# Attention and FFN on one core: unscaled exponentials in the product with the values, inverse sums spread by DMA, and copies on any engine

## The chip, the cores and the metric

The kernel runs on one core of a Trainium2 chip. The metric is the device time of one execution in microseconds (us); lower is better. Times come from runs on the chip, rows from one profiled execution. The engines are TensorE (PE; PEld is its weight load), VectorE (DVE), ScalarE (ACT), GpSimd (POOL) and SyncE (SP), which issues the DMAs.

## The reference

Batch 8, 8 heads, 576 positions, head size 64; all in float32. First attention with a threshold, then an RWKV channel mix on its output `x` (8 x 576 x 512, hidden size 1024):

```python
scores = (1 / sqrt(64)) * (q @ k.T)
scores = where(scores >= max(scores) - tau, scores, -1e9)
attn = exp(scores - max(scores))
attn = attn / (sum(attn) + 1e-9)
x = (attn @ v) by heads, side by side
xk = mu_k * x + (1 - mu_k) * x_prev      # x_prev: x one position later, zero at first
xr = mu_r * x + (1 - mu_r) * x_prev
out = sigmoid(xr @ w_r) * (relu(xk @ w_k) ** 2 @ w_v)
```

## The kernel before

**Jobs.** A job is one batch and one pair of heads: 8 x 4 = 32 jobs. Its queries are taken in 5 units: four of 128 queries of each of the two heads, and one, "T", with the last 64 of both. A unit's scores (PE, L585 and L569) fill 128 x 576 of PSUM, in one of three buffers "s". DVE takes the negated maximum (L631) and adds tau (L639, "bias"); ACT's Prelu with a huge slope (L647, "mask") frees the buffer and leaves every score under the threshold hugely negative; ACT's Exp (L655) gives the exponentials and, by an accumulator, their row sums. DVE adds 1e-9 and inverts (L663, L664), POOL multiplies the rows by the inverses (L678), DVE transposes in 32 x 32 blocks (L695; T: L699), and PE multiplies by the values (L724: 288 matmuls a job, in three pieces, into two "s" buffers). ACT copies the result to `xT` (512 positions) and `xE` (the last 64).

**Split floats.** PE takes `fp32r` operands, so each float32 operand is split into a rounded high half (a copy) and a remainder (a subtraction): ACT copies and POOL subtracts for K (L487, L495), ACT and DVE for Q (L505, L515, which also multiply by 0.125), ACT and POOL for the FFN's inputs (L845, L853) and its squared hidden layer (L888, L898). Weights come as 64-bit words and are turned into floats in four DVE steps (L412 clamp, L426, L433, L443) between ACT copies (L404, L450), with POOL's subtraction (L454).

**FFN.** When a batch's four jobs are done, its 512 positions are two chunks of 256; after batches 3 and 7 the last 64 positions of four batches make a third: 18 chunks. A chunk forms the difference of neighbours (L823), scales it (L832, twice for each of two halves of the channels and each of xk, xr), splits it, and runs 96 matmuls with w_k (L875), 24 with w_r (L917) and 48 with w_v (L939), with relu, square and split between (L883 to L898), a copy and sigmoid for r (L921, L925) and the final product (L945).

**Order.** Nothing is ordered by hand. Each step is added to a `Plan` with its engine, duration, buffers and a key; `Plan.order` simulates all engines and issues whatever can start first, ties by key. Keys are shifted by the tables NUDGE and FIRST. Steps of POOL and those DVE steps listed in PORT are kept from overlapping. The resulting order on each engine is fixed when the kernel is built; an engine waits for its next instruction's inputs even where a later one could run.

Of the kernel before, what the change touches and what calls it, by code (L numbers as in the profile page):

```python
# [7 lines left out]
F32 = mybir.dt.float32  # L8
# [8 lines left out]
TAU = 110.0  # L17
W_MIN = 2.0 ** (0x38 * 2 - 127)
# [24 lines left out]
class Step:  # L43
    __slots__ = (
        "eng", "occ", "lat", "fn", "key", "deps", "succ", "allocs", "idx", "missing", "ready",
        "start", "end", "kb", "soft", "att", "kind", "ni", "after",
# [3 lines left out]
class Plan:  # L50

    HOP, LATE, FROM, AHEAD = 0.05, 0.3, 200.0, 120.0
    SOFT = {"DVE": 0, "ACT": 0}
    NUDGE = {
# [8 lines left out]
    }  # L65
    FIRST, UNTIL = {
# [8 lines left out]
    PORT = {"dve5", "dve6", "dve7", "dve8", "dve7b", "dve14"}  # L75
    CHUNK, FETCH = 256, 3.55

    def __init__(self):
        self.steps = []
        self.tags = {}  # L80
        self.bufs = []

        self.soft = False
# [6 lines left out]
    def add(self, eng, occ, fn, reads=(), writes=(), key=0.0, lat=None, kb=0, wait=0.0, kind=None, ni=0, after=None):  # L90
        s = Step()
        s.soft = self.SOFT.get(eng, 0.0) if self.soft else 0.0
        s.att = eng == "PE" and key < -500
        early = (key + 1000 if s.att else key) < self.UNTIL
        if s.att:
            key += 1000 - self.AHEAD
        s.eng, s.occ, s.fn, s.kb, s.kind, s.ni, s.after = eng, occ, fn, kb, kind, ni, after
        s.key = key + self.NUDGE.get(kind, 0.0) + (self.FIRST.get(kind, 0.0) if early else 0.0)
        s.lat = occ + 0.1 if lat is None else lat
        s.idx = len(self.steps)  # L100
        s.deps, s.succ, s.allocs = set(), [], []
        s.ready = wait
# [36 lines left out]
    def order(self, loose=()):  # L139
        steps = self.steps  # L140
        for s in steps:
# [6 lines left out]
        for b in self.bufs:  # L148
            for u in set(b.users):
# [6 lines left out]
        open_ = {}  # L156
        for s in steps:
            free.setdefault(s.eng, 0.0)
            open_.setdefault(s.eng, set())
        for s in steps:  # L160
            if s.missing == 0:
                open_[s.eng].add(s.idx)
# [26 lines left out]
        while len(out) < total:  # L189
            best = None  # L190
            for e, cand in open_.items():
                f = free[e]
                pick = None
                for i in cand:
# [5 lines left out]
                    if e == "POOL" or s.kind in self.PORT:  # L200
                        t = max(t, port.get("DVE" if e == "POOL" else "POOL", 0.0))
                    late = t + s.soft
                    if s.after is not None:
                        late = max(late, s.after[0].start + s.after[1])
                    k = (late, s.key, i, t)
                    if pick is None or k < pick:
                        pick = k
                if pick is not None and (best is None or pick[0] < best[0]):
                    best = (pick[0], e, pick[2], pick[3])
            if best is None:  # L210
                raise RuntimeError("the plan is stuck")
            _, e, i, t = best
            s = steps[i]
            open_[e].discard(i)
            s.start = t
            if e == "POOL" or s.kind in self.PORT:
                port[e] = t + s.occ
            stall = 0.0
            if s.ni:
                more = self.CHUNK - code % self.CHUNK  # L220
                code += s.ni
                while more <= s.ni:
                    at = t + stall + s.occ * more / s.ni
# [3 lines left out]
            free[e] = t + s.occ + stall  # L227
            if e == "DMA":
                pipe = max(pipe, t) + s.kb / 260.0
                s.end = max(t + 3.5, pipe + 2.5)  # L230
            else:
                s.end = t + s.lat + stall
# [11 lines left out]
            for j in s.succ:  # L244
                n = steps[j]
                n.missing -= 1
                same = n.eng == e and e == "PE"
# [123 lines left out]

# [671 lines left out]
```

## Time and profile before

| | |
|---|---|
| median of 3 runs | 991.8 us (991.47 to 992.29) |
| span of the profiled execution | 992.1 us |
| busy: PE, ACT, DVE, POOL | 896.4, 797.4, 700.8, 576.3 us |
| DMA | 97.48 MB, 31,599 packets |

The span is what a profiled execution shows from its first to its last instruction; no other time is given for that execution, and its span lies within the three runs. Busy time is the union of an engine's instructions, which overlap by some tens of nanoseconds; so the sum of a group's durations is a little more than what it adds to the busy time. A matmul's end is modelled; "idle before" counts only time in which nothing of that engine was under way.

### The profile page before, as it was taken

To read this page: it belongs to the slowest core of one execution; us is meant where nothing else is said; L and a number is where in the kernel's file an instruction comes from. 1 tells how busy PE (TensorE), PEld (TensorE's weight loads), DVE (VectorE), ACT (ScalarE), POOL (GpSimd) and SP (SyncE) were. 2 spreads that over 40 slices of the span, in tenths; PEclk is the share of its full clock that TensorE was granted. 3 is DMA by queue.
4 is the path that set the end of the run, shared out by engine and by line. 5 is a ranking of instruction groups with operands and counts; after the bars stand their busy time and mean duration, and the time that the engine had idled before them with its cause. 6 is when DMAs were issued, how large, how long until landed. Compare 5 with 4: busy or idle time off the path is not lost.

```text
span 992.1 us, 32003 instructions
## 1 busy us (share of the span) xinstructions
PE 896.4 (90%) x13520; PEld 785.9 (79%) x13520; DVE 700.8 (71%) x1434; ACT 797.4 (80%) x1660; POOL 576.3 (58%) x576
## 2 busy tenths in 40 slices
PE   4255668999999999999999999999999999999988
PEld 3154557888888979898989887989888988889876
DVE  6999889886778786878677877696778676731130
ACT  6677897889898988998888888989988888864432
POOL 2556575755676564766666656666575565553431
PEclk9577787999999999999999999999999999999999
DMA  9632232332333233233323232323333321100001
GB/s 339 263 109 75 78 127 63 123 128 84 89 126 109 74 105 116 90 108 96 119 94 122 84 101 91 95 82 98 118 98 107 97 96 62 71 3 22 22 22 22
DMA packets 31599, 97.48 MB, mean 98 GB/s; under 512 B 3808, under 2 KB 3808, under 8 KB 27360
## 3 DMA queue, kind: packets, MB, share of 16 engines
q1 hardware_dynamic: 31456, 95.44, 29.4%
q8 instruction: 106, 1.74, 0.7%
q14 instruction: 37, 0.30, 0.1%
HBM read 85.99 MB, written 9.44 MB: 96 GB/s over the span
## 4 chain that ended last, share of the span: by engine, by line
PE 65%; DVE 16%; ACT 10%; issue 4%; POOL 2%; DMA 2%; SPq 0%; ACTq 0%; POOLq 0%; DVEq 0%
PE w L875 16%; PE s L724 15%; PE w L939 14%; PE s L585 10%; PE w L917 8%; DVE sm L631 4%; ACT sq L647 3%; DVE sq L695 3%; ACT sq L655 3%; PE s L569 3%; DVE r L832 2%; DVE sm L663 1%; DVE qb L515 1%; POOL sq L678 1%; DMA wk<-in_w_k 1%
## 5 line engine op out<-in xcount | busy, mean ns | idle before, releaser
L678 POOL TENSOR_SCALAR sq<-sq,sm 128x576 f32<-128x576 f32 x288 | 233.0, 821 | 166.9 <-DVE sm L664 90.6
L631 DVE TENSOR_REDUCE sm<-s 128x1 f32<-128x576 f32 x288 | 211.5, 746 | 64.7 <-PE s L585 59.0
L647 ACT ACTIVATE sq<-s,sm 128x576 f32<-128x576 f32 x288 | 207.5, 740 | 46.5 <-DVE sm L639 43.9
L875 PE MATMUL w<-xk,wk 128*128 128x256 f32 x1728 | 227.9, 284 | 4.7 <-ACT xk L845 2.3
L655 ACT ACTIVATE sq<-sq,small 128x576 f32<-128x576 f32 x288 | 224.0, 780 | 1.8
L875 PEld LDWEIGHTS w<-xk,wk 128*128 128x128 f32 x1728 | 217.1, 190 | 9.1 <-issue 3.0
L939 PE MATMUL w<-wv,k 128*128 128x512 f32 x864 | 215.6, 394 | 0.0
L695 DVE STREAM_TRANSPOSE sq<-sq 128x1152 f32<-128x1152 f32 x128 | 175.3, 1371 | 40.8 <-POOL sq L678 40.4
L724 PE MATMUL s<-sq,v 32*64 32x144 f32 x9216 | 179.8, 294 | 13.1 <-ACT sq L647 5.0
L724 PEld LDWEIGHTS s<-sq,v 32*64 32x64 f32 x9216 | 151.9, 134 | 40.3 <-issue 20.3
L939 PEld LDWEIGHTS w<-wv,k 128*128 128x128 f32 x864 | 157.0, 188 | 32.3 <-issue 4.0
L585 PE MATMUL s<-kc,qa 128*128 128x288 f32 x512 | 124.2, 326 | 63.1 <-ACT sq L647 41.3
L585 PEld LDWEIGHTS s<-kc,qa 128*128 128x128 f32 x512 | 87.6, 200 | 88.1 <-ACT sq L647 43.7
L853 POOL TENSOR_TENSOR xk<-r,xk 128x512 fp32r<-128x512 f32 x72 | 94.2, 1308 | 80.3 <-ACT xk L845 74.8
L898 POOL TENSOR_TENSOR k<-r,k 128x512 fp32r<-128x512 f32 x72 | 93.7, 1304 | 53.8 <-ACT k L888 53.0
L585 PE MATMUL s<-kc,qb 128*128 128x288 f32 x512 | 115.2, 309 | 3.1 <-DVE qb L515 3.1
L495 POOL TENSOR_TENSOR kc<-rk,kc 64x576 fp32r<-64x576 f32 x64 | 92.8, 1461 | 40.7 <-issue 17.7
L917 PE MATMUL w<-wr,xk 128*128 128x512 f32 x432 | 108.9, 395 | 0.0
L832 DVE SCALAR_TENSOR_TENSOR r<-r,mu_sb,xT 128x256 f32<-128x256 f32 x128 | 65.3, 552 | 37.0 <-POOL xk L853 21.8
L585 PEld LDWEIGHTS s<-kc,qb 128*128 128x128 f32 x512 | 87.2, 200 | 4.6 <-DVE qb L515 3.8
L917 PEld LDWEIGHTS w<-wr,xk 128*128 128x128 f32 x432 | 77.9, 188 | 15.3 <-issue 1.0
L663 DVE TENSOR_SCALAR sm<-sm 128x2 f32<-128x2 f32 (+1 forms) x160 | 47.1, 294 | 53.9 <-ACT sq L655 53.5
(53 smaller groups left out, 914.3 us busy)
## 6 DMA issues: line engine op xcount, KB each, us to landing
v<-in_v SPq DMA_DIRECT2D x32, 1152.0 KB, 5.3
rk<-in_qk SPq DMA_DIRECT2D x64, 288.0 KB, 2.9
rq<-in_qk SPq DMA_DIRECT2D x64, 288.0 KB, 2.9
out<-sg SPq DMA_DIRECT2D x32, 256.0 KB, 2.3
wk<-in_w_k SPq DMA_DIRECT2D x8, 512.0 KB, 9.1
wv<-in_w_v SPq DMA_DIRECT2D x8, 512.0 KB, 10.2
wr<-in_w_r SPq DMA_DIRECT2D x4, 512.0 KB, 8.9
out<-sg SPq DMA_DIRECT2D x8, 128.0 KB, 2.4
```

The source lines that it names most:

```text
L585: PE.matmul(ss[y].get()[:, z, 0:HS], l.get()[:, c * P : (c + 1) * P], r.get()[:, keys(z)], start=(j == 0), stop=(j == 1),)
L631: lambda sv=sv, col=col: V.tensor_reduce(col(0), sv(), axis=AX.XY, op=ALU.max, negate=True),
L647: lambda st=st, pv=pv, col=col: A.activation(pv(), st(), AF.Prelu, bias=col(1), alpha=STEEP),
L655: lambda y=y, col=col: A.activation(part(y), part(y), AF.Exp, bias=small.get()[:, 3:4], accum_out=col(2)),
L678: lambda y=y: G.tensor_scalar(part(y), part(y), sm.get()[:, y, 3:4], 0.0, op0=ALU.mult, op1=ALU.add),
L695: V.transpose(t, t)
L724: PE.matmul(os[a // 2].get()[hs, a % 2, 0:NX], vt.get()[rows, j, hs], sq.get()[rows, j, h], start=(j == 0), stop=(j == NB - 1),)
L853: lambda j=j, d=d, cs=cs: G.tensor_tensor(mix[j].get()[:, 1, cs], d.get(), mix[j].get()[:, 0, cs].bitcast(F32), op=ALU.subtract),
L875: PE.matmul(h.get()[:, f], l, r, start=(ct == 0 and i == 0), stop=(ct == NCT - 1 and i == 2))
L898: lambda r=r, js=js: G.tensor_tensor(k2.get()[:, 1, js], r.get().rearrange("p (a b) -> p a b", a=2), k2.get()[:, 0, js].bitcast(F32), op=A ...
L917: PE.matmul(z.get(), l, r, start=(ct == 0 and i == 0), stop=(ct == NCT - 1 and i == 2))
L939: PE.matmul(vps.get(), l, r, start=(ft == 0 and i == 0), stop=(ft == NFT - 1 and i == 2))
```

## The change

The diff changes some 980 lines; this is its core.

- The exponentials are not normalized. DVE transposes them as they are, PE multiplies them by the values, and the result is multiplied by the inverse sums ("norm", "normt") after its copy from PSUM, once a job. The row sums of a job's 9 score tiles go into one tile `sums`, which starts as ones; one DVE step adds 1e-9, inverts and transposes it. A DMA writes it to DRAM ("line", 128 rows of 128 bytes), and four DMAs read it back so that each of 64 partitions of a head gets that head's inverses along the columns ("lines"). They land in a buffer of tag "raw", which four Q and K loads now share.
- The 0.125 moves from the split of Q to Prelu's `scale` and to the bias step. So Q's high half is a plain copy and its remainder a plain subtraction.
- A step may have several alternatives. Copies may go to ACT, DVE or POOL, two-input steps to POOL or DVE, a copy from PSUM, the relu and the copy for r to ACT or DVE, the clamp of weights and the bias to POOL or DVE; the plan takes whichever can start first, with a penalty for some (PEN), and new tables of keys (by kind and engine, and by job or chunk: GROUP).
- For batch 0 the product with the values fills one "s" buffer and both "w" buffers of the FFN in place of two "s" buffers. The third and later weights are requested by other keys.

```diff
-            add("DVE", 0.2, invert, reads=..., writes=..., key=n + 0.5, lat=0.38, kind="dve11")
-        for y in ys:
-            add("POOL", 0.72,
-                lambda y=y: G.tensor_scalar(part(y), part(y), sm.get()[:, y, 3:4], 0.0, op0=ALU.mult, op1=ALU.add),
...
+                        "bias", 0.11,
+                        lambda col=col, eng=eng: eng.tensor_scalar(
+                            col(1), col(0), SCALE, small.get()[:, 1:2], op0=ALU.mult, op1=ALU.add
...
+                        pv(), st(), AF.Prelu, bias=col(1), scale=SCALE, alpha=STEEP
...
+    def inverse(job, key):
+        total = job["sums"]
+        line = plan.buf(dr, "line", [P, Q], F32, 2)
+        inv = job["inv"] = sbuf("raw", [P, S], F32, NRAW)
+        def invert():
+            t = total.get()
+            V.tensor_scalar(t[:, 0, 0 : 2 * NCQ + 1], t[:, 0, 0 : 2 * NCQ + 1], 1e-9, None, op0=ALU.add)
+            V.reciprocal(t[:, 1, 0 : 2 * NCQ + 1], t[:, 0, 0 : 2 * NCQ + 1])
+            V.transpose(t[:, 1], t[:, 1])
+        add(dve("inv", 0.36, invert, lat=0.6), writes=[total], key=key)
+        add(dma("line", lambda: SY.dma_start(line.get(), total.get()[:, 1]), lat=2.2), reads=[total], writes=[line], ...)
+        for h in range(2):
...
+                SY.dma_start(inv.get()[rows, 0:SM].rearrange("p (a n) -> p a n", a=4), of.broadcast_to([D, 4, P]))
...
+                SY.dma_start(inv.get()[rows, SM:S].rearrange("p (a i) -> p a i", a=4), of.broadcast_to([D, 4, QT]))
...
+        add(pairs("norm", SM, whole, whole, lambda: inv.get()[:, 0:SM].rearrange(...), ALU.mult), ...)
+        add(pairs("normt", ST, end, end, lambda: inv.get()[:, SM:S], ALU.mult), ...)
...
+    def copies(kind, n, to, of, which="AVG"):
+        if "A" in which: r.append(act(kind, 0.094 + 0.000836 * n, lambda: A.activation(to(), of(), AF.Copy)))
+        if "V" in which: r.append(dve(kind, 0.067 + 0.00052 * n, lambda: V.tensor_copy(to(), of()), port=True))
+        if "G" in which: r.append(pool(kind, 0.08 + 0.00111 * n, lambda: G.tensor_scalar(to(), of(), 1.0, 0.0, ...)))
+    def pairs(kind, n, to, a, b, op, which="GV"):
+        if "G" in which: r.append(pool(kind, 0.08 + 0.00228 * n, lambda: G.tensor_tensor(to(), a(), b(), op=op)))
+        if "V" in which: r.append(dve(kind, 0.067 + 0.00104 * n, lambda: V.tensor_tensor(to(), a(), b(), op=op), port=True))
```

The tables move nearly every instruction. Three places show how.

DVE, in the first stage, around the fifth and sixth scale instruction on xT (L832), which feed the first FFN matmuls; before (L663 and L664 invert sums, L515 is Q's remainder, L639 the bias):

```order
L663 TENSOR_SCALAR sm_1437<-sm_1437 128x2
L664 RECIPROCAL sm_1437<-sm_1437 128x2
L631 TENSOR_REDUCE sm_1588<-s_1568 128x1
L631 TENSOR_REDUCE sm_1588<-s_1590 128x1
L639 TENSOR_SCALAR sm_1588<-sm_1588,small 128x1
L631 TENSOR_REDUCE sm_1611<-s_1598 128x1
L639 TENSOR_SCALAR sm_1588<-sm_1588,small 128x1
L639 TENSOR_SCALAR sm_1611<-sm_1611,small 128x1
L832 SCALAR_TENSOR_TENSOR r_1624<-r_1604,mu_sb,xT_68 128x256 x2
L515 SCALAR_TENSOR_TENSOR qb_1636<-rq_1075,small,qa_1576 128x576
L515 SCALAR_TENSOR_TENSOR qb_1639<-rq_1348,small,qa_1596 128x576
L631 TENSOR_REDUCE sm_1611<-s_1619 128x1
```

The same two scale instructions (L997) in the change; L709 is the maximum, L720 the bias, L407 a copy, L424 a two-input step, L781 to L783 a job's inversion:

```order
L720 TENSOR_SCALAR sm_1574<-sm_1574,small 128x1
L424 TENSOR_TENSOR xE<-xE,raw_1308 128x64
L980 TENSOR_TENSOR r_1585<-xT_70 128x512
L407 CAST kc_1589<-raw_1515 128x576
L997 SCALAR_TENSOR_TENSOR r_1591<-r_1585,mu_sb,xT_70 128x256 x2
L424 TENSOR_TENSOR kc_1589<-raw_1515,kc_1589 64x576
L407 CAST xk_1016<-r_1591 128x512
L709 TENSOR_REDUCE sm_1612<-s_1596 128x1
L709 TENSOR_REDUCE sm_1619<-s_1577 128x1
L781 TENSOR_SCALAR sums_76<-sums_76 128x9
L782 RECIPROCAL sums_76<-sums_76 128x9
L783 STREAM_TRANSPOSE sums_76<-sums_76 128x32
```

The pairs of inversions are gone, one triple stands for a whole job, and DVE now copies and subtracts for K, scales `xE` by the inverses, forms the difference and makes the high half of xk itself.

POOL, up to the low half of xk that the first FFN matmuls wait for (L853), before; L678 normalizes:

```order
L495 TENSOR_TENSOR kc_1579<-rk_1283,kc_1579 64x576
L823 TENSOR_TENSOR r_1604<-xT_68 128x512
L771 TENSOR_SCALAR xE<-xT_68 128x4
L678 TENSOR_SCALAR sq_1317<-sq_1317,sm_1437 128x18x32 x2
L495 TENSOR_TENSOR kc_1608<-rk_1323,kc_1608 64x576
L678 TENSOR_SCALAR sq_1317<-sq_1317,sm_1588 128x18x32 x2
L853 TENSOR_TENSOR xk_1213<-r_1624,xk_1213 128x512
```

The same low half (`xk_1016`, L422) in the change; L494 clamps weights:

```order
L422 TENSOR_TENSOR qb_1544<-raw_1391,qa_1540 128x576
L422 TENSOR_TENSOR xT_70<-xT_70,raw_1308 128x4x4x32
L413 TENSOR_SCALAR bd<-qb_1544 128x4x16
L422 TENSOR_TENSOR wv_0_1551<-xT_72,wv_0_1551 128x512
L494 TENSOR_SCALAR xT_72<-xT_72 128x512
L422 TENSOR_TENSOR xk_1016<-r_1591,xk_1016 128x512
```

Normalizing is gone from POOL; a scaling by the inverses (`xT_70<-xT_70,raw_1308`), Q's remainders and clamps are there in its place.

SP, the issues of one job's inverses in the change (there were none before), with the raw loads behind them:

```order
L792 DMA line_1290<-sums_80 128x32
L803 DMA raw_1308<-line_1290 64x4x128
L807 DMA raw_1308<-line_1290 64x4x16
L803 DMA raw_1308<-line_1290 64x4x128
L807 DMA raw_1308<-line_1290 64x4x16
L553 DMA raw_1373<-in_qk 128x576
L553 DMA raw_1382<-in_qk 128x576
```

The first waits for DVE's inversion, the second for the first to land, and the loads of Q and K are issued after both.

## Rows read from the trace of the kernel before

**Rows 1.** The page's part 1: busy us, share, instructions.
```profile
PE 896.4 (90%) x13520; PEld 785.9 (79%) x13520; DVE 700.8 (71%) x1434; ACT 797.4 (80%) x1660; POOL 576.3 (58%) x576
```

**Rows 2.** Busy time by stage (us from the start; instructions), granted clock, DMA.
```profile
0.00:157.60 157.60, 81.88 (x1380) 68.77 (x1381) 138.24 (x269) 118.86 (x254) 86.80 (x85) 0.72 0.46 162
...
175.00:870.00 695.00, 683.53 (x10895) 600.98 (x10882) 522.36 (x1069) 614.79 (x1296) 434.16 (x438) 1.00 0.31 99
...
917.00:992.00 75.00, 66.60 (x375) 58.44 (x373) 13.63 (x44) 23.84 (x38) 24.46 (x25) 0.96 0.07 22
```

**Rows 3.** PE's waits, 0 to 175 us: total, times, longest.
```profile
PE s L585 <- ACT sq L647: 39.3, 17, 11.6
```

**Rows 4.** Timeline around the first FFN matmul: start, us, instruction.
```profile
146.26 1.78 DVE L832 SCALAR_TENSOR_TENSOR r<-r,mu_sb,xT 128x256 f32<-128x256 f32 x2
148.27 0.62 ACT L845 ACTIVATE xk<-r 128x512 fp32r<-128x512 f32 x1
153.54 1.26 POOL L853 TENSOR_TENSOR xk<-r,xk 128x512 fp32r<-128x512 f32 x1
157.63 1.48 PE L875 MATMUL w<-xk,wk 128*128 128x256 f32 x6
```

**Rows 5.** DVE by line, 0 to 148 us: busy us, mean ns, idle before.
```profile
L631 DVE TENSOR_REDUCE sm<-s 128x1 f32<-128x576 f32 x46 | 33.9, 748 | 8.9 <-PE s L585 5.7 <-PE s L569 3.0
L515 DVE SCALAR_TENSOR_TENSOR qb<-rq,small,qa 128x576 fp32r<-128x576 f32 x12 | 11.8, 987 | 5.0 <-ACT qa L505 5.0
L412 DVE TENSOR_SCALAR xT<-xT 128x512 f32<-128x512 f32 x17 | 9.8, 590 | 0.4 <-ACT xT L404 0.3
L639 DVE TENSOR_SCALAR sm<-sm,small 128x1 f32<-128x1 f32 x46 | 9.1, 202 | 0.3
L443 DVE SCALAR_TENSOR_TENSOR xT<-wk,xT 128x512 uint32<-128x512 uint32 x8 | 8.2, 1020 | 0.0
L663 DVE TENSOR_SCALAR sm<-sm 128x2 f32<-128x2 f32 (+1 forms) x24 | 6.3, 263 | 0.3
L664 DVE RECIPROCAL sm<-sm 128x2 f32<-128x2 f32 (+1 forms) x24 | 4.0, 167 | 0.8
```

**Rows 6.** The tile xT on DVE, 0 to 160 us: ns, shortest, median, longest.
```profile
L426 DVE TENSOR_SCALAR xT<-xT x17: 405/422/1498, 13.2 to 139.8; 128x512 uint32<-128x512 uint32 x17
L433 DVE SCALAR_TENSOR_TENSOR xT<-wk,xT x8: 675/683/1114, 15.0 to 54.6; 128x512 uint32<-128x512 uint32 x8
```

**Rows 7.** Groups by line over the whole span: busy us, mean ns, idle before.
```profile
L678 POOL TENSOR_SCALAR sq<-sq,sm 128x576 f32<-128x576 f32 x288 | 233.0, 821 | 166.9 <-DVE sm L664 90.6 <-DVE sm L639 25.8 <-ACT sq L655 9.9
L515 DVE SCALAR_TENSOR_TENSOR qb<-rq,small,qa 128x576 fp32r<-128x576 f32 x64 | 58.5, 926 | 5.0 <-ACT qa L505 5.0
L663 DVE TENSOR_SCALAR sm<-sm 128x2 f32<-128x2 f32 (+1 forms) x160 | 47.1, 294 | 53.9 <-ACT sq L655 53.5
L945 DVE TENSOR_TENSOR sg<-w,sg 128x512 f32<-128x512 f32 x36 | 24.5, 680 | 49.0 <-issue 32.9 <-PE w L939 16.0
```

**Rows 8.** Timeline at 36 us, a pass of POOL and one of DVE.
```profile
36.48 1.59 POOL L454 TENSOR_TENSOR wk<-xT,wk 128x512 fp32r<-128x512 f32 x1
36.87 1.49 DVE L426 TENSOR_SCALAR xT<-xT 128x512 uint32<-128x512 uint32 x1
```

**Rows 9.** The chain of waits, four long pieces of PE: start, us, line.
```profile
882.50 1.71 PE s L724 x96
897.85 11.48 PE w L875 x96
909.33 5.50 PE w L917 x24
976.67 10.89 PE w L939 x48
```

**Rows 10.** The page's part 6: DMA issues, KB each, us to landing.
```profile
v<-in_v SPq DMA_DIRECT2D x32, 1152.0 KB, 5.3
out<-sg SPq DMA_DIRECT2D x8, 128.0 KB, 2.4
```

More of the change, by code (lines that the diff above doesn't have):

```diff
@@ L246, in order @@
                 n.missing -= 1
-                same = n.eng == e and e == "PE"
+                same = e == "PE" and n.alts[0][0] == "PE"
                 late = self.LATE if n.att and t > self.FROM else 0.0
-                n.ready = max(n.ready, t + s.occ + stall if same else s.end + self.HOP + late)
+                n.ready = max(n.ready, t + occ + stall if same else s.end + self.HOP + late)
                 if n.missing == 0:
-                    open_[n.eng].add(j)
+                    release(n)
             out.append(i)
@@ new lines, in dma @@
+    def dma(kind, fn, lat=3.5):
+        return ("DMA", DQ, lat, fn, kind, False)
+    def copies(kind, n, to, of, which="AVG"):
+        r = []
+        if "A" in which:
+            r.append(act(kind, 0.094 + 0.000836 * n, lambda: A.activation(to(), of(), AF.Copy)))
+        if "V" in which:
+            r.append(dve(kind, 0.067 + 0.00052 * n, lambda: V.tensor_copy(to(), of()), port=True))
+        if "G" in which:
+            r.append(
+                pool(
+                    kind,
+                    0.08 + 0.00111 * n,
+                    lambda: G.tensor_scalar(to(), of(), 1.0, 0.0, op0=ALU.mult, op1=ALU.add),
+                )
+            )
+        return r
@@ L359, in tile_threshold_attention_then_rwkv_ffn @@
+    add(dve("tau", 0.4, threshold), reads=[(small, 0)], writes=[(small, 1), (small, 3)], key=-1000)
     mu_sb = fixed("mu_sb", [P, 2, NCT])
@@ L711, in attend, with bank @@
         tail = [(xE, (b % NE, hp))]
-        os = [psum("s", [P, 2, 512], 3) for _ in range(2)]
         last = job["units"][-1]
-        for o in os:
-            add("PE", 0.0, lambda: None, reads=[(last["sm"], (RES, 1))], writes=[o, *main, *tail], key=-400.0, lat=0.0, kind="pe4")
+        if job["ji"] < NPAIR:
+            os = [psum("s", [P, 2, 512], 3), *(psum("w", [P, 512], NF) for _ in range(2))]
+            groups = [(os[0], 0, 2), (os[1], 2, 1), (os[2], 3, 1)]
+        else:
+            os = [psum("s", [P, 2, 512], 3) for _ in range(2)]
+            groups = [(os[0], 0, 2), (os[1], 2, 2)]
+        def bank(o, z):
+            return o.get()[:, z] if o.tag == "s" else o.get()
+        where = {a + z: (o, z) for o, a, m in groups for z in range(m)}
+        for o in os:
+            add(
+                pe("hold", 0.0, lambda: None, lat=0.0),
+                reads=[(last["sm"], (1, 1))],
+                writes=[o, *main, *tail],
+                key=-400.0,
+            )
         for k in range(KC):
@@ new lines, in attend, with whole, end @@
+        inv = job["inv"]
+        def whole():
+            return rows(x.get()[:, hp, 1 : 1 + SM])
+        def end():
+            return xE.get()[:, hp, b % NE, 1 : 1 + ST]
+        add(
+            pairs(
+                "norm",
+                SM,
+                whole,
+                whole,
+                lambda: inv.get()[:, 0:SM].rearrange("p (a c i) -> p a c i", a=4, i=Q),
+                ALU.mult,
+            ),
+            reads=[(inv, (0, h)) for h in range(2)],
+            writes=main,
+            key=key - 5,
+        )
@@ L767, in edge @@
+        add(
+            pairs("normt", ST, end, end, lambda: inv.get()[:, SM:S], ALU.mult),
+            reads=[(inv, (1, h)) for h in range(2)],
+            writes=tail,
+            key=key - 5,
+        )
     def edge(b, key):
         add(
-            "POOL",
-            0.16,
-            lambda: G.tensor_scalar(
-                xE.get()[:, :, b % NE, 0:1], xT[b % 2].get()[:, :, SM : SM + 1], 1.0, 0.0, op0=ALU.mult, op1=ALU.add
+            copies(
+                "edge",
+                NCT,
+                lambda: xE.get()[:, :, b % NE, 0:1],
+                lambda: xT[b % 2].get()[:, :, SM : SM + 1],
@@ new lines, in two @@
+            def two(r=r):
+                return r.get().rearrange("p (a b) -> p a b", a=2)
+            add(
+                [
+                    act("relu", 0.478, lambda r=r, flat=flat: A.activation(r.get(), flat(), AF.Relu), lat=0.6),
+                    dve("relu", 0.6, lambda r=r, flat=flat: V.tensor_scalar(r.get(), flat(), 0.0, None, op0=ALU.max)),
+                ],
+                reads=[h],
+                writes=[r],
+                key=key - 20,
+            )
+            add(
+                [
+                    act("sqr", 0.52, lambda r=r: A.activation(r.get(), r.get(), AF.Square)),
+                    *pairs("sqr", 512, lambda r=r: r.get(), lambda r=r: r.get(), lambda r=r: r.get(), ALU.mult),
+                ],
+                writes=[r],
+                key=key - 1,
+            )
```

712 lines of the change are left out of this document (415 added, 297 removed), and 29 rows, old and new, of tables (GROUP, NUDGE).

## The prediction

> **What bounds the kernel now.** I read the page's shares first, then busy time by stage, then TensorE's (PE's) waits, then VectorE (DVE) alone in the first stage. PE is busy 90% of the span, ScalarE (ACT) 80%, DVE 71%, GpSimd (POOL) 58% [rows 1]; such an average hides where PE stands still. By stage [rows 2]: up to 157.6 us, where the first FFN matmul of xk with w_k starts, DVE is busy 138.2 us of 157.6 (88%) and PE 81.9, at a mean granted clock of 0.72. From 175 to 870 PE is busy 683.5 of 695, so it stands still for 11.5 us; beside it ACT works 614.8 (88%) and DVE 522.4 (75%). After 870 only FFN chunks are left, and PE is still idle for 8.4 of the last 75. So PE sets the time after the start; in the start the softmax chain does. The longest waits there say it: PE waits 39.3 us for the ACT mask to free a score bank [rows 3], and ACT got its bias from a DVE with little time to spare. By PE's order 228 score matmuls (0.13 us each: 288 columns against the 256 of L875, which take 0.12 [rows 9]) and 1,152 of the product with the values (0.018 each [rows 9]) lie ahead of the first FFN matmul: 50 us of work spread over 157.6. That is the place to win.
>
> **The start, on DVE.** Up to the sixth "scale" instruction on xT (L832; it ends at 148.0, [rows 4]) the order before and the order now hold nearly the same work on DVE: 46 maxima, 18 + 5 transposes, 16 weight tiles' last two steps. So only the difference counts, priced from DVE's own rows up to 148 us [rows 5]. Removed: 24 pairs of sum and reciprocal, 6.3 + 4.0 us; 11 fused q remainders at 987 ns, 10.9; 15 of 17 weight clamps, which go to POOL, at 590 ns, 8.9; 9 of 46 biases, also to POOL, at 202 ns, 1.8. Together 31.9.
> Added, between the shortest and the longest price that a like row shows:
> - 9 copies (7 of 576 columns, 2 of 512). A one-input pass over 512 columns takes 422 ns at the median [rows 6] and 589 on average [rows 5]: 4.1 to 5.8.
> - 7 two-input passes over 512 columns (5 weight remainders, a difference, a scaling by the inverses): 683 ns at the median [rows 6] to 950, just under the 1020 of the dearest row [rows 5]: 4.8 to 6.7.
> - 7 of 576 columns (k and q remainders): 770 ns, the 683 scaled up, to 987: 5.4 to 6.9.
> - 4 triples that invert a whole job's sums, like the 263 + 167 ns of a pair plus one more small step: 1.9 to 2.8.
> - 4 scalings of 64 tail columns at 202 to 294 ns, like the small passes [rows 5, 7]; 4 copies out of PSUM, one of 256 and three of 128 columns, at 680 ns per 512 [rows 7] or half as much again: together 1.6 to 2.5.
> The sum is 17.8 to 24.7, so DVE is rid of 7 to 14 us. I take 11, nearer the good end, because POOL has less to do and collides less (below). The scale ends at 137 instead of 148.
>
> **From the scale to the first FFN matmul** before took 9.6 us, 148.0 to 157.6. POOL formed the low half only at 153.54 [rows 4]; in its order a k remainder and two normalizing passes stood ahead. Now a clamp alone stands ahead, and DVE makes the high half itself. At best it takes 0.8 + 0.4 + 1.3 = 2.5 us (a k remainder, the copy, POOL's 1.26), at worst 9.6 again. I take 4, near the low end, since what stood ahead is gone; PE's own row of score matmuls keeps it from less. The first FFN matmul comes at 141: **17 us earlier**. Eight score matmuls fewer lie ahead of it (220, 228 before), at 0.13 us each: 1 us back.
>
> **After it** PE has the same 13,520 matmuls in all. What moves is beside it. POOL loses its 288 normalizing passes, 233 us [rows 7]. Its two-input passes stay near their number (276 before, 263 now, 1.3 us each: 17 us less); 106 biases (21 us at DVE's 202 ns) and some 70 one-input passes at up to 821 ns (57 us) are new: 576 - 233 - 17 + 21 + 57 = 404. ACT hands some 340 of its copies, relus and squares on; at 0.6 us [rows 4] that is up to 200 of its 797. DVE gains: it loses 47 us of sums [rows 7] and 27 of reciprocals (160 at 167 ns [rows 5]), 58.5 of fused q remainders [rows 7], 21 of biases and 10 of clamps, and gets about 70 + 44 copies, 103 + 54 two-input passes and 54 + 36 reads of PSUM, by the prices above 240 to 286 us. So DVE goes from 701 to 776 to 823, and becomes the busiest engine after PE, near the 88% at which ACT stands there now. One nearly full neighbour takes the place of another: I take 3 of the 11.5 idle us (between all of them, and as many again lost). At the end the scaling by the inverses adds a step of 0.7 to 1.3 us ahead of the last batch's mix, while its halves may go to three engines: 2 us won, bounds 8 won and 5 lost. The DMAs (5 more a job, 160 in all) are costed at nothing: SP is no bound, and attention's own product covers them; if that cover is too short, see the third rival.
> **Sum:** 992.1 - 17 + 1 - 3 - 2 = **971 us**, 955 to 985 by these bounds when they don't all fall on one side. The profiled span, 992.1, lies within the three runs (991.47 to 992.29, median 991.8), so no correction.
>
> **A rule against it.** A DVE pass that began at 36.87 ended at 38.36, 0.29 us after POOL's pass that began at 36.48 [rows 8]; alone it takes 0.42 [rows 6]. It stood still for as long as POOL worked. The Trainium skill ("SBUF — State Buffer", Who interferes with whom) says why: DVE copies in a two-port mode, and DVE passes with two SBUF inputs, share a port pair with GpSimd, and the loser waits for the other's whole instruction. By that rule the two loads add up. POOL's falls by 172; such DVE passes grow by 122 to 168 (the 240 to 286, less some 50 of PSUM reads, less 58.5 + 10 removed). So the rule leaves the sum where it is, and only speaks against the place: POOL can wait, DVE can't. That is the second rival.
>
> **Rivals.**
> 1. *PE gains in the long stage too.* At the rates of undisturbed pieces (96 of L875 in 11.48 us, 24 of L917 in 5.50, 48 of L939 in 10.89, 96 of L724 in 1.71 [rows 9], scores 0.13) the matmuls from the first FFN matmul on need 207 + 99 + 196 + 144 + 137 = 783 us; they took 834.5. If ACT at 88% cost half of those 52: 992 - 16 - 26 = **950**. Against it: only 20 us show as idle, the rest lies inside rows of busy PE that this change leaves alone.
> 2. *Slower: collisions on DVE.* Some 580 DVE passes may now stand behind POOL (336 before), 520 of them ahead of the last maximum. At the shortest prices DVE's 776 us, less some 60 that its order now puts behind that maximum, are 716; with 19 idle in the start (157.6 - 138.2), today's 870 us are reached once each pass waits 0.26 us on average. For it: weight rows average 0.34 over their median (1020 against 682) [rows 5, 6]. Against it: POOL works 30% less, and by the median rows most passes wait for nothing. At 0.30 the stage ends at 716 + 156 + 19 = 891, 21 later than now: **1013**.
> 3. *The inverses come late.* They go to DRAM and back: a store of 128 KB lands in 2.4 us, a v tile in 5.3 [rows 10], so 5 to 8 us in all; behind the waiting issue stand the next raw loads on SP. In PE's order only 5 to 9 us of work stand between the end of attention and the first FFN matmul for batches 0, 3, 6 and 7. Five late us at each of the four: 971 + 20 = **991**. Against it: a job's product alone is 288 matmuls, 5.1 us at the rate of rows 9, and is issued in three pieces with other work between, all after the sums are known. The Trainium skill ("DMA: Bandwidth & Descriptors", Specifications) adds that pieces under 512 B cost a read-modify-write; the new rows are of 64 to 512 B, and no row here prices that.
> 4. *The start doesn't shrink*, as loads of weights and the chain max, bias, mask, exp set it and not DVE's sum: 4 us of 17 remain, **984**. For it: DVE's maxima wait 8.9 us there, mostly for PE [rows 5]. Against it: the other 138 us DVE is busy.
>
> **Chances.** Forecast 0.55; rivals 1 to 4: 0.20, 0.09, 0.06, 0.10. The range, 943 to 992, takes in rivals 1, 3 and 4 and leaves rival 2 and a little of both ends out. About 0.2%, 2 us, is what a measurement tells from no change: faster by more 0.87 (forecast, 1, 4 and a third of 3), within 0.04, slower by more 0.09.
>
> **What will show it.** Right: the first w_k matmul at about 141 us with DVE still near 88% busy before it; POOL near 404 us in all, ACT near 620, DVE near 800; PE idle in the long stage 10 us or less; no wait of a norm pass for a DMA on the chain. Wrong: w_k starting after 150 (rival 4), copies and remainders on DVE averaging 0.25 us over 0.42 and 0.68 (rival 2), PE or POOL waiting for the inverses' DMA (rival 3), PE's stage from its first FFN matmul to the end under 815 us (rival 1).

## The result: 0.7% slower

The changed kernel takes 1000.5 us (median of 10 runs, 993.8 to 1004.2) beside 992.5 for the kernel before (10 runs, 991.0 to 994.1): a ratio of 1.0069, 95% interval 1.0050 to 1.0089. The forecast was 971, the range ended at 992. The profiled execution spans 1000.6 us.

The page's part 1 of the changed kernel, and its busy time on either side of the first matmul with w_k (columns as in [rows 2]):

```profile
PE 906.1 (91%) x13520; PEld 793.5 (79%) x13520; DVE 791.0 (79%) x1445; ACT 642.1 (64%) x1321; POOL 408.1 (41%) x467
```
```profile
0.00:134.30 134.30, 78.65 (x1373) 65.69 (x1374) 117.61 (x217) 100.84 (x222) 63.58 (x78) 0.76 0.54 186
134.30:1000.60 866.30, 827.41 (x12149) 727.77 (x12148) 673.37 (x1229) 541.25 (x1101) 344.54 (x390) 0.98 0.31 95
```

The neighbours of PE carry what was forecast, and the start shrank by more than forecast: 134.3 us instead of 157.6 [rows 2]. All of that and more is lost behind it. The kernel before needed 834.5 us there (992.1 - 157.6), with PE busy for 814.5 (896.4 - 81.9, [rows 1, 2]); now it is 866.3, with PE busy for 827.4. So PE stands still for 19 us more and takes 13 us longer for the same matmuls, 12,149 of them here and 12,141 before. What PE waits for (whole span: total, times, longest):

```profile
PE s L847 <- issue: 28.4, 19, 4.1
PE s L652 <- ACT sq L734: 25.1, 20, 5.0
PE w L847 <- issue: 3.7, 2, 2.3
PE w L1149 <- issue: 2.7, 1, 2.7
```

"issue" is idle time for which the profile shows no wait: 34.8 us in all, 2.4 in the kernel before. Nearly all of it falls on L847, the product with the values. One such stall on PE's timeline, with score matmuls and w_k matmuls on both sides of it:

```profile
192.95 0.53 PE L652 MATMUL s<-kc,qa 128*128 128x288 f32 x2 [0.32 <-ACT sq L734]
193.32 0.42 PE L652 MATMUL s<-kc,qb 128*128 128x288 f32 x2
193.58 0.87 PE L1046 MATMUL w<-xk,wk 128*128 128x256 f32 x6
194.38 1.68 PE L847 MATMUL s<-sq,v 32*64 32x144 f32 x82
200.13 0.78 PE L847 MATMUL s<-sq,v 32*64 32x144 f32 x14 [4.07 <-issue]
200.84 0.85 PE L652 MATMUL s<-kc,qa 128*128 128x288 f32 x2
201.49 0.68 PE L652 MATMUL s<-kc,qb 128*128 128x288 f32 x2
201.97 1.27 PE L1046 MATMUL w<-xk,wk 128*128 128x256 f32 x5
```

PE stops in the middle of a piece of 96 and goes on 4 us later. Then it is slow as well: two score matmuls take 0.85 us instead of 0.53, five of w_k 1.27 where six took 0.87. The granted clock says why, 1.00 before the stall, 0.65 on average over the stall and the microseconds behind it, and 0.50 right behind it (last columns: granted clock, DMA share, GB/s). Of the chip's two levels, 2.4 and 1.2 GHz, PE was given the lower one for a time after it had stood still, so this stall is paid for twice:

```profile
186.00:196.00 10.00, 9.62 (x212) 8.02 (x212) 9.47 (x15) 8.31 (x18) 2.31 (x5) 1.00 0.46 118
196.00:204.00 8.00, 3.93 (x49) 3.26 (x56) 3.02 (x5) 1.39 (x4) 1.66 (x2) 0.65 0.37 108
200.13:204.00 3.87, 3.87 (x48) 3.26 (x56) 1.79 (x2) 0.56 (x1) 0.26 (x1) 0.50 0.05 14
```

What came just before, on SP's timeline (start, us to issue, line, DMA):

```profile
187.82 0.33 SPq L792 DMA_DIRECT2D line<-sums  x1
189.28 0.59 SPq L803 DMA_DIRECT2D raw<-line  x1
189.97 1.49 SPq L553 DMA_DIRECT2D raw<-in_qk  x3
191.51 0.59 SPq L807 DMA_DIRECT2D raw<-line  x1
192.14 0.74 SPq L803 DMA_DIRECT2D raw<-line  x1
192.93 0.93 SPq L807 DMA_DIRECT2D raw<-line  x1
193.91 1.18 SPq L1171 DMA_DIRECT2D out<-sg  x2
```

L792 stores a job's inverses, L803 and L807 spread them, L553 loads Q or K rows of the next job. SP waited for the sums, stored, waited again for the store to land, and then sent nine loads or stores more within 6 us. PE's instructions come over the same DMA engines, as queue q8. The DMA queues from 174 to 197 us (packets, MB, share) and, in the second fence, from 197 to 204:

```profile
q1 hardware_dynamic: 1861, 2.57, 37.3%
q14 instruction: 1, 0.01, 0.1%
```
```profile
q1 hardware_dynamic: 370, 0.54, 24.5%
q8 instruction: 2, 0.03, 2.4%
```

No packet of q8 ran from 174.9 to 197.2 us; then one did, up to 198.7, and PE went on at 200.1. Such a gap alone proves nothing: without the store and the loads (e_nodma, below) q8 is silent from 169.2 to 188.3, and PE has no stall put down to issue there. PE's own count does. q8 moved 106 packets of 16,384 bytes and PE ran 27,147 instructions (matmuls, weight loads, semaphore steps), 256 to a packet. Counted in their order in the trace, 21 of the 22 stops put down to issue, 33.7 of the 34.8 us, lie where one piece of 256 ends and the next begins, and each of the 15 of these that last over 1 us ends 1.2 to 1.5 us behind the end of a q8 packet. Other runs show the same: 4.5 of 5.6 us lie there in e_nodma, 11.2 of 12.2 in c_ldact5. So in these stalls PE waits for its own instructions. PE began the piece before the stall above at 191.76, and the packet with the next piece began only at 197.21; in between the DMA engines were 95% busy (last column but one):

```profile
191.76:197.21 5.45, 3.98 (x149) 3.31 (x135) 4.96 (x8) 3.71 (x9) 0.53 (x2) 1.00 0.95 261
```

Six more stalls of over 2 us behind this one follow the same cluster on SP. The DMA issues of the whole span (KB each, median us to landing), and SP's waits (total, times, longest):

```profile
raw<-in_qk SPq DMA_DIRECT2D x128, 288.0 KB, 4.9
raw<-line SPq DMA_DIRECT2D x64, 128.0 KB, 4.8
raw<-line SPq DMA_DIRECT2D x64, 16.0 KB, 4.9
```
```profile
SPq L792 <- DVE sums L783: 248.5, 28, 17.8
SPq L553 <- DMA raw<-in_qk: 33.1, 16, 4.3
SPq L803 <- DMA line<-sums: 32.5, 26, 2.8
```

Rows of Q and K now land in 4.9 us; in the kernel before in 2.9. DVE, ACT and POOL wait 47.4 us for them in all (15.4 before), the longest two groups here:

```profile
ACT qa L405 <- DMA raw<-in_qk: 18.6, 10, 3.7
DVE qa L407 <- DMA raw<-in_qk: 15.8, 9, 3.6
```

No engine but SP waits for the inverses or for their store.

### The profile page after: what moved, and what is told of

Its sections match the earlier page's. It is cut to its first block, busy times and chain, and to the rows that moved or that the text cites. A ratio compares the mean times of both kernels' runs of the same rounds, so it can differ in the third digit from the quotient of the medians.

```text
span 1000.6 us, 31601 instructions
## 1 busy us (share of the span) xinstructions
PE 906.1 (91%) x13520; PEld 793.5 (79%) x13520; DVE 791.0 (79%) x1445; ACT 642.1 (64%) x1321; POOL 408.1 (41%) x467
## 4 chain that ended last, share of the span: by engine, by line
PE 73%; DVE 15%; issue 5%; ACT 4%; DMA 2%; POOL 1%; SPq 1%; DVEq 0%; ACTq 0%; POOLq 0%
PE w L1046 18%; PE w L1149 17%; PE s L847 15%; PE s L652 11%; PE w L1115 8%; DVE sm L709 4%; DVE sq L762 3%; PE s L630 3%; DMA raw<-in_qk 2%; ACT sq L734 2%; ACT sq L746 1%; DVE xT L527 1%; DVE kc L424 1%; PE w L847 1%; DVE kc L407 1%
## 5 line engine op out<-in xcount | busy, mean ns | idle before, releaser
L709 DVE TENSOR_REDUCE sm<-s 128x1 f32<-128x576 f32 x288 | 209.7, 746 | 43.7 <-PE s L652 33.7
L847 PE MATMUL s<-sq,v 32*64 32x144 f32 x8640 | 189.9, 295 | 30.8 <-issue 28.4
L847 PEld LDWEIGHTS s<-sq,v 32*64 32x64 f32 x8640 | 156.4, 134 | 60.6 <-issue 50.8
L762 DVE STREAM_TRANSPOSE sq<-sq 128x1152 f32<-128x1152 f32 x128 | 173.6, 1362 | 11.6 <-ACT sq L746 11.5
L652 PE MATMUL s<-kc,qa 128*128 128x288 f32 x512 | 123.2, 324 | 43.8 <-ACT sq L734 25.1
L422 POOL TENSOR_TENSOR xk<-r,xk 128x512 fp32r<-128x512 f32 x72 | 98.2, 1364 | 156.5 <-DVE xk L407 114.3
L652 PEld LDWEIGHTS s<-kc,qa 128*128 128x128 f32 x512 | 90.5, 202 | 65.6 <-ACT sq L734 28.9
L652 PE MATMUL s<-kc,qb 128*128 128x288 f32 x512 | 116.0, 310 | 0.0
L1115 PE MATMUL w<-wr,xk 128*128 128x512 f32 x432 | 111.3, 399 | 0.0
L652 PEld LDWEIGHTS s<-kc,qb 128*128 128x128 f32 x512 | 87.8, 201 | 1.3 <-issue 1.2
L422 POOL TENSOR_TENSOR qb<-raw,qa 128x576 fp32r<-128x576 f32 x39 | 56.0, 1436 | 48.2 <-ACT qa L405 24.2
L997 DVE SCALAR_TENSOR_TENSOR r<-r,mu_sb,xT 128x256 f32<-128x256 f32 x128 | 60.2, 511 | 18.5 <-POOL xk L422 17.4
L720 POOL TENSOR_SCALAR sm<-sm,small 128x1 f32<-128x1 f32 x106 | 28.8, 273 | 102.2 <-DVE sm L709 92.9
L422 POOL TENSOR_TENSOR kc<-raw,kc 64x576 fp32r<-64x576 f32 x35 | 51.2, 1462 | 30.6 <-DVE kc L407 9.7
L1127 ACT ACTIVATE sg<-w 128x512 f32<-128x512 f32 x27 | 16.0, 594 | 72.2 <-PE w L1115 72.2
```

Of the source, the lines that this page charges most:

```text
L422: r.append(pool(kind, 0.08 + 0.00228 * n, lambda: G.tensor_tensor(to(), a(), b(), op=op)))
L652: PE.matmul(ss[y].get()[:, z, 0:HS], l.get()[:, c * P : (c + 1) * P], r.get()[:, keys(z)], start=(j == 0), stop=(j == 1),)
L709: lambda sv=sv, col=col: V.tensor_reduce(col(0), sv(), axis=AX.XY, op=ALU.max, negate=True),
L762: V.transpose(t, t)
L847: PE.matmul(bank(*where[a])[hs, 0:NX], vt.get()[rows, j, hs], sq.get()[rows, j, h], start=(j == 0), stop=(j == NB - 1),)
L997: V.scalar_tensor_tensor(d.get()[:, y, o : o + n], diff.get()[:, y, o : o + n], mu_sb.get()[:, j, hc + y : hc + y + 1], prv[:, hc + y], op ...
```

## The experiments

All kernels but the three named b_ are the changed one with an edit of its DMAs; on PE, DVE, ACT and POOL they keep its order of work, but for the instructions that an edit names. "Issue" is PE's idle time put down to issue, "rows" the time that DVE, ACT and POOL wait for Q and K rows, both in us of one profiled execution; the ratio is to the kernel before, run beside it on the same chip.

| run | edit | us | ratio (95%) | issue | rows |
|---|---|---|---|---|---|
| changed kernel | | 1000.5 | 1.0069 (1.0050 to 1.0089) | 34.8 | 47.4 |
| e_nodma | no store, no loads | 961.5 | 0.9695 (0.9669 to 0.9721) | 5.6 | 2.4 |
| e_store | store alone | 963.8 | 0.9705 (0.9675 to 0.9735) | 9.6 | 2.6 |
| e_free | loads alone | 962.6 | 0.9705 (0.9673 to 0.9736) | 7.3 | 7.1 |
| e_noland | both, no wait between them | 973.1 | 0.9826 (0.9788 to 0.9864) | 17.1 | 16.3 |
| e_fat | loads in long rows | 974.3 | 0.9828 (0.9786 to 0.9870) | 18.5 | 29.3 |
| e_rows | 5 stores, 2 loads in long rows | 988.1 | 0.9964 (0.9948 to 0.9980) | 17.5 | 72.3 |
| c_quad | 3 stores, long rows, 4 transposes | 992.8 | 1.0012 (0.9990 to 1.0035) | 15.5 | 25.8 |
| c_act | store and loads from ACT | 976.3 | 0.9837 (0.9808 to 0.9865) | 10.7 | 4.2 |
| c_ldact | loads from ACT | 973.6 | 0.9800 (0.9770 to 0.9831) | 13.0 | 6.9 |
| c_ldact5 | the same again | 971.8 | 0.9790 (0.9772 to 0.9807) | 12.2 | 6.2 |
| e_ldactfat | loads from ACT in long rows | 968.9 | 0.9756 (0.9724 to 0.9789) | 11.5 | 7.3 |
| c_actrows | e_rows, all from ACT | 1018.6 | 1.0265 (1.0239 to 1.0291) | 2.7 | 5.6 |

**First: is it the DMAs at all, and which property?** The theory was that their many small pieces hold up the loads of PE's instructions; its rivals, that PE's new order bunches the product by itself, and that SP waits for the sums and then sends everything at once, whatever the pieces.

e_nodma:
```diff
-    dma("line", lambda: SY.dma_start(line.get(), total.get()[:, 1]), lat=2.2),
-    SY.dma_start(inv.get()[rows, ...]...)   # four times a job
-    norm: x times inv
+    norm: x times x
```


> The change without any store or load of inverses; the scaling step multiplies the attention's output by itself, at the same size, so the scaling by the inverses is left out. Same order on PE, DVE, ACT and POOL. Theory 1: issue idle under 8 us, time 964 to 976. Theory 2: issue idle near 35 and 998 to 1002. Theory 3: SP no longer waits for the sums, 966 to 980. So this tells theory 2 from the others, and e_fat tells 1 from 3.

961.5 us, 39 less than the changed kernel (37 by the ratios): the spreading of the inverses costs more than the whole loss, and PE's new order alone bunches nothing. The two stretches of this run:

```profile
0.00:129.00 129.00, 78.60 (x1372) 67.17 (x1373) 116.61 (x217) 100.92 (x221) 63.05 (x78) 0.74 0.52 188
129.00:959.40 830.40, 814.06 (x12150) 718.68 (x12148) 672.66 (x1229) 539.48 (x1101) 342.90 (x390) 1.00 0.26 88
```

e_fat:
```diff
-    of = line...[:, :, NCQ * h * Q : NCQ * (h + 1) * Q]    # 4 pieces of 512 bytes a partition, and 4 of 64
+    of = line.get().rearrange("(o r) i -> o (r i)", o=1)[:, 0:SM]    # 1 piece of 2048, and 1 of 256
```


> The change with each load of inverses as one row a partition: 64 pieces of 2,048 bytes and 64 of 256 bytes in place of 256 of 512 and 256 of 64, twice a job; same bytes, same number of issues, same waits, same order on all engines. The values it spreads are not the inverses, so this leaves the right scaling out. Theory 1 (the many small pieces hold up PE's instruction loads): PE's idle time put down to issue falls from 35 us to under 10, the raw loads land in 3 to 4 us rather than 4.9, time 970 to 980. Theory 2 (PE's order bunches the product's pieces, so that it asks for instructions faster than they can come, whatever the DMAs do): issue idle stays near 35, time 998 to 1002. Theory 3 (SP waits for the sums and then issues loads in a burst; the number of bytes and issues counts, not that of pieces): issue idle 25 to 35, time 992 to 1001.

e_rows:
```diff
-    SY.dma_start(line.get(), total.get()[:, 1])
+    for a in range(4): SY.dma_start(line[:, a * P : (a + 1) * P]..., t[a * Q : a * Q + 2 * NCQ, 1])
+    SY.dma_start(line[:, SM:S]..., t[2 * NCQ :: Q, 1]...)
-    four loads of pieces of 512 and 64 bytes
+    SY.dma_start(inv.get()[rows], line.get()[h : h + 1].broadcast_to([D, S]))    # twice
```


> The change with the inverses stored so that each head's 576 lie in a row in DRAM: five small stores a job (40 pieces in all) and two loads of 64 pieces of 2,304 bytes, in place of one store of 128 pieces and four loads of 1,024. Computes all of the reference. Same order on PE, DVE, ACT and POOL. Theory 1: issue idle under 10 us, time 966 to 980, faster than the kernel before by 1 to 2.5%. Theory 2: 998 to 1002. Theory 3: six to seven issues a job remain in the same places, 990 to 1001.

b_small, the kernel before with four loads a job of 512 pieces in all per head (256 of 320 bytes, 256 of 64), nobody reading them:
```diff
-    lambda: SY.dma_start(vt.get(), v[b, hp]...),
+    lambda: (SY.dma_start(vt.get(), v[b, hp]...), extra(b, hp)),
```


> The kernel before, with four further loads a job, into a tile that nothing reads, issued right behind the load of the values: twice 256 pieces of 320 bytes and 256 of 64 bytes, as many pieces as the change has. Same order on all other engines. Theory 1: PE's issue idle rises from 2 to over 8 us, time 995 to 1012. Theory 2: nothing changes, 991 to 994. Theory 3: 991 to 995, since SP waits for nothing new.

b_small took 991.9 us, ratio 1.0009 (0.9994 to 1.0025), issue 2.4: as many small pieces as in the change cost nothing behind the load of v. So their number alone decides nothing. Long rows at the changed kernel's place won some 25 us (e_fat: 974.3), though SP waits for the sums there as before; so SP's wait alone doesn't either. e_rows, with the fewest pieces, won only some 11 (988.1): five stores a job make the Q and K rows later still, 72.3 us of waits for them.

**Second: wait or pieces?**

e_store keeps the store, e_free the loads, from the rows of Q and K:
```diff
# e_store
-    SY.dma_start(inv.get()[rows, ...]...)   # four times a job; norm: x times x
# e_free
-    dma("line", lambda: SY.dma_start(line.get(), total.get()[:, 1]), lat=2.2),
-    of = line...
+    of = qk[job["b"], job["hp"], h, 0:4, 0:P]...    # and 0:QT
```


> The changed kernel with the store of the inverses kept, so that SP still waits for each job's sums and for the store's buffer, but with its four loads left out; the norm passes multiply x by itself (the output is not the reference's). Theory A, that the loads' many small pieces, issued right when a job's sums are done, are what costs: close to the kernel without store and loads, 959 to 968 us, PE's idle time put down to issue at most 9 us. Theory B, that SP's wait for the sums is what costs, since it holds up the loads of the next job's rows and sends them in a burst: 975 to 1000 us, issue idle above 15 us.

> The changed kernel without the store: the four loads of a job stay at their places in SP's queue with the same pieces (512 and 64 bytes), but read the input rows, so that SP waits for no sums; the values are not the inverses. Theory A: the pieces still travel with the loads of the next job's rows, so 980 to 1000 us and issue idle above 15 us; lower within that the more the loads drift away from the product. Theory B: without the wait nothing bunches, 960 to 970 us, issue idle at most 9 us.

Both 963 us. In e_store SP waits for the sums as long as in the changed kernel; in e_free the same pieces go, in the same order on SP. Each alone costs 1 to 2 us over e_nodma, together they cost 39. Neither run has the second wait, that of the loads for the store to land, since that takes both. Both theories failed as they were put: A in e_free, B in e_store (whose issue idle, 9.6 us, lies a little above A's bound of 9).

b_hot is the kernel before with the change's store and loads behind each job's last inverse; b_hotfat the same in long rows:
```diff
     V.reciprocal(sm.get()[:, ysl, 3], sm.get()[:, ysl, 2])
+    if unit is unit["job"]["units"][-1]: extra(unit["job"], sm.get())    # copy, store, four loads
```


> The kernel before with a store of 128 rows and four loads of small pieces (256 of 288 bytes and 256 of 64 bytes, twice) per job, issued right behind the last inverse of a job's sums, the place that they have in the change; nobody reads them. Theory A (place and pieces) and theory B (SP's wait) both: 1000 to 1025 us, with PE's issue idle above 10 us. Theory C, that only the changed kernel's own order of work is open to it: 990 to 995 us and issue idle at most 4 us, as with the loads behind the v load.

> The kernel before with the same store and four loads per job at the same place as in the run with small pieces there (1003 us), but each load in long rows (64 of 1152 bytes and 64 of 256 bytes, twice). If SP's wait and the five DMAs cost, the number of pieces being of no account: 1000 to 1005 us. If the pieces cost: 990 to 997 us.

1003.3 us (ratio 1.0114, 1.0092 to 1.0136) and 1004.8 (1.0112, 1.0088 to 1.0136). Here the five DMAs with SP's waits cost 11 us whatever the pieces, and issue idle rises only to 5.7 and 5.8 us, not above 10. By the profiles b_hot is 8.9 us longer (1001.0 and 992.1): 1.6 lie in the start (its first w_k matmul comes at 159.2), 2.4 in PE standing still behind it and 4.9 in slower matmuls. What slowed these isn't settled.

c_quad computes all of the reference: four transposes into one block of partitions, so that long rows need three stores.
```diff
-    V.transpose(t[:, 1], t[:, 1])
+    for a in range(4): V.transpose(t[0:Q, 2 + a], t[a * Q : (a + 1) * Q, 1])
```


> The changed kernel with whole inverses in long rows and right values: four 32x32 transposes into one block of 32 partitions in place of one, a store of 8 rows of 512 bytes and two stores of 4 times 64 bytes, then four loads of long rows (64 of 2048 bytes, 64 of 256 bytes, twice). Theory A: 970 to 980 us, issue idle 14 to 20 us, as with the long rows of other values. Theory B: the two stores more lengthen SP's wait, 983 to 992 us, as with five stores.

992.8 us, a little above what B said, but not for B's reason alone: the four transposes cost as much on DVE as a large one each (its row of DVE's groups by duration: shortest, median, longest ns), 25.6 us in place of 6.8, and DVE's busy time rises to 811.9 us. This run mixes two causes and settles neither.

```profile
L784 DVE STREAM_TRANSPOSE sums<-sums x128: 199/200/204, 28.0 to 883.7; 32x32 f32<-32x32 f32 x128
```

**Third: take it out of SP's queue.**

c_act lets ACT's queue issue store and loads, c_ldact the loads alone:
```diff
-    SY.dma_start(inv.get()[rows, 0:SM]...)    # and [rows, SM:S]
+    A.dma_start(inv.get()[rows, 0:SM]...)
# c_act also
-    SY.dma_start(line.get(), total.get()[:, 1])
+    A.dma_start(line.get(), total.get()[:, 1])
```


> The changed kernel with the store of the inverses and their four loads issued by ACT's queue in place of SP's, everything else and every value the same: SP no longer waits for sums, ACT waits for DVE's inverses and for the store to land. Theory D, which the last runs leave: neither the pieces nor the wait costs by itself, but in SP's one queue the wait holds back the next job's row loads, so that they go together with the small pieces, at the moment when the product draws PE's instructions. D: the row loads go early again, issue idle falls below 15 us and the time to 962 to 978 us. Theory A, that the pieces just then are enough: 985 to 1000 us, issue idle above 20 us. Rival E: ACT's own waits hold up the mask and exponential passes, and PE waits for them: 980 to 1010 us with PE's waits for ACT above 25 us behind 175 us.

> The changed kernel with the four loads of the inverses on ACT's queue, as in the 976 us run, but with the store left in SP's, so that SP waits for a job's sums again before it gets to the next row loads. Theory D, that SP's wait holds back the row loads until they go together with the small pieces: 985 to 1002 us, row loads landing in 4.5 us or more, issue idle above 18 us. Theory F, that it is the loads' place in SP's queue, between the row loads, which then go through one queue behind the small pieces: 972 to 980 us and issue idle at most 13 us, as with all of them on ACT.

> The five small stores and two loads of long rows (the 988 us run), all issued by ACT's queue; right values. If the pieces still cost there: 964 to 974 us, issue idle at most 8 us. If ACT's waits and issues take the gain back: 976 to 990 us, with PE's waits for ACT's mask passes above those of the run with small pieces on ACT (7.6 us behind 175 us).

976.3 and 973.6 us; both compute all of the reference, and both are faster than the kernel before and the changed one. In c_ldact SP still waits for the sums, so D fell and F held: what matters is that the loads, and the wait for the store to land, stand in SP's queue ahead of the Q and K rows. c_actrows (e_rows, its stores and loads all from ACT) has hardly any issue idle left (2.7 us) and is the slowest of all, above either expectation: ACT, which has passes to run, waits for the stores to land, and PE for ACT's mask passes (25.4 us at L652 behind 175 us, 7.6 in c_act). Its rows of ACT's waits:

```profile
ACT sq L746 <- DMA line<-sums: 27.8, 10, 3.5
ACT sq L734 <- DMA line<-sums: 10.3, 3, 4.7
```

**Last: the wait for landing, or the queue?** e_noland is e_free with the store kept: SP waits for the sums, but the loads behind read rows of Q and K and so don't wait for the store. e_ldactfat is e_fat with its loads on ACT's queue.

> The changed kernel with its store kept on SP (which waits for the sums) and the four loads behind it, the same pieces, but reading the input rows, so that SP doesn't wait for the store to land; the values are not the inverses. F1, that this second wait holds the row loads back until they go with the pieces: 964 to 977 us, issue idle at most 14 us. F2, that small pieces ahead of the row loads in one queue are enough: 985 to 1000 us, issue idle above 20 us.

> Store on SP, the four loads on ACT's queue and in long rows (64 of 2048 and 64 of 256 bytes, twice; they spread values that are not the inverses). If pieces cost in a queue of their own too: 962 to 968 us, issue idle at most 10 us. If what is left there (974 us) is the waits and not the pieces: 971 to 976 us, issue idle 11 to 15 us.

> The kernel with the store on SP and the four loads on ACT's queue once more, with right values, in five rounds: 970 to 977 us, a ratio to before of 0.978 to 0.984.

e_noland took 973.1 us: with the same pieces in the same queue, some 25 us go with the wait for landing (F1), so small pieces ahead of the rows are not enough (against F2). Issue idle, 17.1 us, stayed above F1's bound of 14, and some 12 us over e_nodma remain. That its loads read input rows and not the stored line isn't what saves: c_ldact reads the line and takes 973.6. e_ldactfat, 968.9 us, lies between its two expectations: in a queue of their own the pieces cost a few us at most (0.9756 beside 0.9790). c_ldact5, the kernel of c_ldact once more and the fastest here that computes all of the reference, took 971.8 us. At the place of the stall above, the same part of its PE timeline and the DMA queues from 174 to 197 us:

```profile
189.99 1.68 PE L847 MATMUL s<-sq,v 32*64 32x144 f32 x82
191.85 0.50 PE L847 MATMUL s<-sq,v 32*64 32x144 f32 x14 [0.19 <-issue]
192.28 0.53 PE L652 MATMUL s<-kc,qa 128*128 128x288 f32 x2
```
```profile
q1 hardware_dynamic: 1021, 1.84, 25.2%
q10 hardware_dynamic: 1088, 0.30, 5.9%
q8 instruction: 3, 0.05, 1.0%
```

PE breaks off after the same 82 matmuls, at the same place between two pieces of 256 instructions, for 0.19 us instead of 4.07, and q8 got its packets in time. SP issued the three Q and K rows 0.4 us behind the store, while that was still under way, and ACT the small pieces from 184.3 to 190.9 (ACT's queue is q10).

## Why the prediction was wrong

- **The step that failed** is one sentence: "The DMAs (5 more a job, 160 in all) are costed at nothing: SP is no bound, and attention's own product covers them". The product covers the inverses' landing: nobody waits for them. It doesn't cover what they push aside. By e_nodma the price is 39 us, and by the profiles 41 (1000.6 - 959.4): 5 of it in the start (134.3 - 129.0), 22.6 of PE standing still behind it (38.9 - 16.3) and 13.4 of slower matmuls (827.4 - 814.1). From 175 to 870 us PE stood still for 32.1 us (695.0 - 662.9), where the prediction looked for 10 or less; without the DMAs it is 10.2.
- **The rest of the sum held, but for the size of one term.** Without the DMAs the part behind the first w_k matmul takes 830.4 us; the forecast, 971 - 141, is 830. The terms of +1, -3 and -2 are right together. The start, forecast at -17, came out at -23 with the DMAs and -29 without. On DVE the working held. Up to the end of the sixth scale instruction, where it stops, DVE was rid of 13.5 us (129.4 - 115.9), near the good end of its 7 to 14, and of the 40 instructions that it counted (254 and 214; before and then the change, columns as in [rows 2]):

```profile
0.00:148.04 148.04, 76.36 (x1362) 64.29 (x1363) 129.40 (x254) 112.09 (x237) 81.77 (x81) 0.73 0.47 166
0.00:132.50 132.50, 77.16 (x1366) 64.43 (x1367) 115.86 (x214) 99.04 (x217) 63.10 (x77) 0.76 0.55 188
```

The scale ended at 132.5 instead of the forecast 137, as 2 us of DVE's idle time went as well, which the sum took as fixed. From there to the first w_k matmul it took 1.8 us, where the prediction took 4 and held 2.5 for the least: that matmul began at 134.3, before POOL had ended the low half at 135.1.

- **The engines** went where they should: POOL 408 us (404), ACT 642 (620), DVE 791 (800). DVE was busy for 88% of the start, as said.
- **Rival 2, collisions on DVE**, didn't come. The means of copies and two-input passes of 512 and 576 columns (groups by line and shape) lie at most 0.10 us over their prices (422 and 683 ns, scaled up for 576 columns); the "wrong" sign was 0.25. Three of the groups:

```profile
L424 DVE TENSOR_TENSOR k<-r,k 128x512 fp32r<-128x512 f32 x38 | 27.5, 724 | 2.8 <-ACT k L405 2.0
L407 DVE CAST xk<-r 128x512 fp32r<-128x512 f32 x38 | 16.2, 426 | 1.3
L407 DVE CAST kc<-raw 128x576 fp32r<-128x576 f32 x25 | 14.0, 561 | 2.3 <-DMA raw<-in_qk 2.2
```

- **Rival 3, the inverses come late**, named the place (the next raw loads stand on SP behind the waiting issue) and the wrong victim: not PE or POOL waiting for the inverses, but PE waiting for its own instructions and ACT and DVE for Q. So it was priced at 20 us and given 0.06. That pieces under 512 B cost a read-modify-write, the page's rule that rival 3 quoted (the Trainium skill, "DMA: Bandwidth & Descriptors", Specifications), isn't what decides here: e_free sends the same pieces, b_small as many, at no cost that can be measured, 962.6 beside 961.5 us and a ratio of 1.0009.
- **Rivals 1 and 4**: PE's part from its first FFN matmul was 830 us even without the DMAs, not under 815; and the start did shrink.

What stays argued: that "issue" is PE waiting for its instructions is shown by the count above; that the packets of q8 come late because the DMA engines are full is not. It rests on the 95% beside the stall and on the stalls shrinking in every run that thins or spreads the traffic there; no run changed the instruction loads themselves. Another rule of the Trainium skill bears on it (the same page, Queues, rings and completion order): each DMA engine takes turns between the queues, a packet at a time. By it a load of q8 would get through behind one packet of q1. The 5.45 us until the late packet began speak neither for it nor against it, since no row says when PE asked for one. And c_quad, e_rows and b_hot each hold some us whose place or cause isn't settled.

## What to carry to other kernels

A DMA whose data nobody waits for can still be dear, through what stands behind it in the same queue and through what shares the DMA engines with it. Before costing a store and the loads behind it at nothing, ask who issues the next loads, and whether that queue will now wait twice, for the data and for the landing, and send all that piled up just when PE runs through its instructions fastest. Loads that wait for a store to land belong in a queue with nothing urgent behind them: here ACT's queue for the four loads (the engine's name in two lines) turns 0.7% slower into 2.1% faster. ACT's queue isn't free either: with five stores a job in it as well (c_actrows) ACT waits for their landing, and the kernel is 2.7% slower than before.

## What the runs showed of the hardware

- PE's instructions arrive in 106 packets of queue q8 over the same DMA engines, 256 instructions to a packet. In the product with the values, 96 matmuls and their weight loads in 1.7 us, PE can run dry between two packets: stalls of up to 4.1 us, 33.7 us in all beside 2.3 in the kernel before.
- Of the seven stalls of over 2 us behind the start, five were followed by matmuls at a granted clock below 1 (0.50 from 200.13 to 204.00 us). Behind the other two, of 2.66 and 2.16 us, it was 1.00 (397.34 to 405.00 and 854.34 to 862.00).
- Two costs that are next to nothing alone (2 us for the store with SP's wait, 1 for the loads) made 39 together, with the wait for the store to land between them; without that wait (e_noland) they made 12.
- Four DVE transposes of 32 x 32 take 200 ns each, one of 128 x 32 takes 211.
